# Query heads split one step ahead, and two small matmul groups set behind a denominator

## The chip, the cores and the metric

One core of a Trainium2 chip runs the whole program. The metric is device time in microseconds (us) of one execution; lower is better. PE is TensorE, ACT ScalarE, DVE VectorE, POOL GpSimd; SP only issues DMAs here. Each engine works through its own queue in order, and the engines wait for each other through semaphores.

## The reference, cut to what matters

```python
proj = q @ w_phi;  proj -= max(abs(proj), axis=-1)          # per head, 128 features
q_p = concat([exp(proj), exp(-proj)]);  k_p likewise
kv, z = k_p.T @ v, sum(k_p)                                 # per batch and head
x = (q_p @ kv) / (q_p @ z + 1e-6)                           # attention, 2304 tokens x 512
xn = x / sqrt(mean(x*x) + 1e-6) * rms_g
y = (silu(xn @ w_gate) * (xn @ w_val)) @ w_out              # feed-forward of width 1536
logits = y @ phi                                            # 32 slots
d = softmax of logits over tokens;  c = softmax over slots
slot_in = d.T @ y;  out = c @ experts(slot_in)              # soft mixture of 8 experts
```

## The kernel before

The work comes in three stages. In the first (to about 210 us) the keys are turned into features and `kv` and `z` are summed. The second is the feed-forward layer over six blocks of 384 tokens, and nearly all that the change touches lies in it. The third (from about 708 us) is the experts and the output.

In the second stage a block has 12 steps m. A step has three runs of matmuls on PE: the gate `pg` (12 matmuls of 384 columns), the value `pv` (12 again), and the output of the step before, `acc` (9 of 512 columns). After each of the three runs `fill()` is called; it runs whatever a list, `plan`, holds for that slot. So slot 3m lies behind the gate, slot 3m+1 behind the value, slot 3m+2 behind the output. Two kinds of work are put into these slots, by tables of numbers at the top of the file:

- `REDUCED` places the steps of `Reduced`, which makes the attention output of the next block (for blocks 2 to 5, so while blocks 1 to 4 run). Per head h: `split` (ACT casts the raw query to `qx`, DVE puts the remainder into the lower half), `feature` (two matmuls `qP`, an ACT copy into `qe`, a POOL maximum over the partitions), `exps` (DVE subtracts, ACT takes two exponentials). Per pair of heads c: `attend` (matmuls `num` with 64 columns of weights and `den` with 32, on DVE the reciprocal of `den`, eight small ACT copies that spread it, the product, the squares added into `s`). At the end `scale`: `ssq`, six passes of PE over `s`, then a reciprocal root on DVE, a sum on POOL, and `out`, whose result `xraw` is cast and split into `xnh` and `xnl` for the gate of the next block.
- `PSLOTS` places the nine steps of `post` for the block before: three turns `x2tp`, `logits` (`LT`, 32 columns of weights), `rows` (`L`), `dturn` (`dtp`), `dispatch` (`sps`, 32 columns), `combine` (DVE and ACT), `cturn` (`ctp`, then the copy `cb` on DVE and a DMA).

All of `qP`, `num`, `den`, `ssq`, `x2tp`, `LT`, `L`, `dtp`, `sps` and `ctp` take turns in three PSUM buffers of one tag. A framework compiles the program and may move an instruction some places forward or back on its engine; the order that comes out of it is quoted below. At the beginning `qx` has one buffer and `qraw` two, and `split(h + 1)` is written behind the matmuls of head h.

Of the kernel before, what the change touches and what calls it, by code (L numbers as in the profile page):

```python
# [7 lines left out]
F32 = mybir.dt.float32  # L8
F32R = mybir.dt.float32r
# [12 lines left out]
BLK = 384  # L22
# [6 lines left out]
NLEFT = 2  # L29
ELEFT = 4  # L30
CSKIP = 5
PSLOTS = [1, 4, 7, 10, 13, 15, 17, 19, 23]
REDUCED = [0, 0, 2, 3, 5, 6, 4, 8, 7, 11, 12, 9, 14, 12, 17, 18, 15, 20, 18, 23, 24, 26, 29]
TURNED0 = [2, 8, 14, 20, 12, 15, 20, 26, 28, 31]
TURNED1 = [0, 7, 14, 21, 6, 13, 20, 26, 28, 30]

# [25 lines left out]
def tile_kernel(ctx: ExitStack, tc: tile.TileContext, q2T, qT, kT, v, wbd, wg, wv, wo, rmsg, phi, w1, w2, consts, out):  # L62
# [34 lines left out]
    def split(hi, lo, src, hi_eng=None, lo_eng=None):  # L97

        if hi_eng is ACT:
            ACT.copy(out=hi, in_=src)  # L100
        else:
            (hi_eng or DVE).tensor_copy(hi, src)
        (lo_eng or POOL).tensor_tensor(out=lo, in0=src, in1=hi.bitcast(F32), op=ALU.subtract)  # L103
# [7 lines left out]
    class Conv:  # L111
# [6 lines left out]
        def load(self):  # L118
            j, nm, c = self.key
            self.raw = self.sp.tile([128, 512, 2], U32, tag="wraw", name="wraw", bufs=self.bufs[0])  # L120
            SP.dma_start(out=self.raw.rearrange("p n w -> p (n w)"), in_=wsrc[nm][j, :, 512 * c:512 * c + 512].bitcast(U32))
# [15 lines left out]
        def parts(self):  # L137
            j, nm, c = self.key
            if (nm, j) not in W:
                W[nm, j] = (wpA if j < 3 else wpool["B"]).tile([128, 2, 1024], F32R, tag="w", name=f"w{nm}{j}")  # L140
            u = W[nm, j]
            s = slice(512 * c, 512 * c + 512)
            split(u[:, 0, s], u[:, 1, s], self.w, hi_eng=ACT, lo_eng=POOL)
# [119 lines left out]
    class Reduced(Q):  # L263


        def load(self, h):
            if h < NH:
                self.raw[h] = self.sp.tile([128, BLK], F32, tag="raw", name="qraw", bufs=2)
                SP.dma_start(out=self.raw[h], in_=qT[self.blk - 2, h])

        def split(self, h):

            if h < NH:
                x = self.x[h] = self.sp.tile([128, BLK], F32R, tag="x", name="qx", bufs=1)
                ACT.copy(out=x, in_=self.raw[h])
                DVE.tensor_tensor(out=x[64:128], in0=self.raw[h][64:128], in1=x[64:128].bitcast(F32), op=ALU.subtract)  # L276

        def feature(self, h):
            x = self.x.pop(h)
            p = self.psum("qP", [128, BLK])  # L280
            PE.matmul(out=p, lhsT=ws, rhs=x, start=True, stop=False)  # L281
            PE.matmul(out=p, lhsT=wl, rhs=x, start=False, stop=True)
            e = self.e[h] = self.sp.tile([128, 2, BLK], F32, tag="e", name="qe", bufs=3)
            ACT.copy(out=e[:, 1], in_=p)  # L284
            POOL.partition_all_reduce(e[:, 0], e[:, 1], channels=128, reduce_op=bass_isa.ReduceOp.absmax)  # L285
            self.split(h + 1)
            self.load(h + 3)

        def exps(self, h):
            e = self.e[h]  # L290
# [10 lines left out]
            return r  # L301

        def begin(self):
            self.load(0)
            self.load(1)

        def steps(self):
            def first():
                self.split(0)
                self.load(2)  # L310

            f = [lambda h=h: self.feature(h) for h in range(NH)]
            a = [lambda c=c: self.attend(c) for c in range(4)]
            g = [lambda h=h: self.exps(h) for h in range(NH)]
            s = [first, *(x for c in range(4) for x in (f[2 * c], f[2 * c + 1], g[2 * c], g[2 * c + 1], a[c])), self.scale, self.out]
            return sorted(zip(REDUCED, s), key=lambda x: x[0])

    class Turned(Q):
# [7 lines left out]
        def split(self, c):  # L326
            if c < 4:
                xh = self.sp.tile([128, BLK], F32R, tag="xh", name="qxh", bufs=1)
                xl = self.sp.tile([128, BLK], F32R, tag="xl", name="qxl", bufs=1)
                split(xh, xl, self.raw[c], hi_eng=ACT)  # L330
                self.x = xh, xl
                self.load(c + self.bufs["raw"])
# [55 lines left out]
    with ExitStack() as pk:  # L388
# [5 lines left out]
        class Front:  # L394
# [10 lines left out]
            def split(self, hf):  # L405
                xh = self.sp.tile([128, 2, 128], F32R, tag=self.tag + "xh", name="xh", bufs=self.bufs["x"])
                xl = self.sp.tile([128, 2, 128], F32R, tag=self.tag + "xl", name="xl", bufs=self.bufs["x"])
                split(xh, xl, self.raw[:, 2 * hf:2 * hf + 2], hi_eng=ACT, lo_eng=DVE if self.i < 2 else POOL)
                self.x[hf] = xh, xl
# [225 lines left out]
    with ExitStack() as p2:  # L635
# [230 lines left out]
        for blk in range(NBLK):  # L866
# [25 lines left out]
            for n, f in qsteps:  # L892
                plan[n].append(f)
            for n, f in zip(PSLOTS, steps):
                plan[n].append(f)
# [189 lines left out]
```

## Time and profile before

| what | us |
|---|---|
| median of 3 runs (lowest, highest) | 775.92 (774.70, 778.17) |
| the profiled execution | 774.93 |
| its span, first to last instruction | 773.1 |
| PE busy in the span | 725.2 (94%) |
| DVE busy | 457.0 (59%) |
| ACT busy | 373.1 (48%) |
| POOL busy | 160.1 (21%) |

The granted TensorE clock over the whole span is 0.987. The share of PE is a mean over the three stages; what a wait in the second stage costs has to be read there. A matmul's record is longer than its distance from the next one, since matmuls overlap: a 384-column matmul is recorded with 0.34 us, and twelve follow each other in 2.12 us in the chain.

### The profile page before, as it was taken

The numbers are of one execution on the slowest core, as the hardware profiler recorded it, in microseconds if no ns is written. First come the engines' busy times: TensorE is split into PE (matmuls) and PEld (weight loads), VectorE is DVE, ScalarE is ACT, GpSimd is POOL, SyncE is SP. The second block draws the span as 40 slices with busy tenths as digits, with TensorE's granted clock in tenths as the row PEclk, the third lists the DMA queues.
The fourth block names the chain that finished last, engine by engine and source line by source line (L and its number), as shares of the span: only waits on it lengthen the run. The fifth ranks groups of instructions, "written<-read, shape, count | busy, mean of one in ns | idle before, by whom it ended". The sixth has DMA issues, their size and how long they took to land.

```text
span 773.1 us, 12571 instructions
## 1 busy us (share of the span) xinstructions
PE 725.2 (94%) x4871; PEld 580.3 (75%) x4871; DVE 457.0 (59%) x875; ACT 373.1 (48%) x867; POOL 160.1 (21%) x128
## 2 busy tenths in 40 slices
PE   6997899977899999999999999999999999999895
PEld 4664555966698887888878898789887899988343
DVE  6898777889956556455565555655556453423313
ACT  6889775565644455534555345553455531212102
POOL 2662330446610211012110121101211010000000
PEclk9999999999999999999999999999999999999899
DMA  8763311544201100101000010000100045667798
GB/s 282 246 209 101 125 42 50 194 137 162 84 23 36 32 21 21 46 1 32 21 20 19 1 32 22 22 19 1 32 21 1 8 162 216 222 218 284 285 374 289
DMA packets 27739, 79.47 MB, mean 103 GB/s; under 512 B 2976, under 2 KB 13664, under 8 KB 23584
## 3 DMA queue, kind: packets, MB, share of 16 engines
q1 hardware_dynamic: 27456, 77.79, 29.4%
q10 hardware_dynamic: 224, 0.88, 0.4%
q8 instruction: 38, 0.62, 0.3%
q14 instruction: 21, 0.17, 0.1%
HBM read 71.99 MB, written 6.67 MB: 102 GB/s over the span
## 4 chain that ended last, share of the span: by engine, by line
PE 65%; DVE 5%; ACT 4%; issue 1%; POOL 1%; DMA 0%; ACTq 0%; POOLq 0%; SPq 0%; DVEq 0%
PE pv L826 18%; PE pg L826 15%; PE acc L851 6%; PE acc L852 5%; PE acc L853 5%; PE num L213 3%; PE y L960 2%; PE y L976 2%; PE den L221 2%; ACT qe L231 1%; ACT e L231 1%; PE x2tp L654 1%; PE qP L281 1%; DVE qx L276 1%; DVE xraw L232 1%
## 5 line engine op out<-in xcount | busy, mean ns | idle before, releaser
L826 PE MATMUL pg<-xnh,wg 128*128 128x384 f32 x576 | 151.6, 343 | 0.9 <-ACT xnh L100 0.5
L826 PE MATMUL pv<-xnh,wv 128*128 128x384 f32 x576 | 151.1, 343 | 1.0 <-DVE t L838 1.0
L826 PEld LDWEIGHTS pg<-xnh,wg 128*128 128x128 f32 x576 | 104.5, 189 | 9.9 <-DVE hl L103 3.4
L826 PEld LDWEIGHTS pv<-xnh,wv 128*128 128x128 f32 x576 | 102.9, 188 | 6.7 <-issue 5.2
L285 POOL PARTITION_ALL_REDUCE qe<-qe x32 | 49.5, 1547 | 258.6 <-ACT qe L284 239.0
L826 PE MATMUL pg<-xnl,wg 128*128 128x384 f32 x288 | 97.7, 339 | 0.0
L826 PE MATMUL pv<-xnl,wv 128*128 128x384 f32 x288 | 97.7, 339 | 0.0
L851 PE MATMUL acc<-wo,hh 128*128 128x512 f32 x216 | 88.6, 410 | 2.1 <-ACT hh L100 2.1
L853 PE MATMUL acc<-wo,hl 128*128 128x512 f32 x216 | 85.8, 397 | 0.4 <-POOL hl L103 0.4
L852 PE MATMUL acc<-wo,hh 128*128 128x512 f32 x216 | 85.9, 398 | 0.0
L834 DVE SCALAR_TENSOR_TENSOR t<-t,pg 128x384 f32<-128x384 f32 x72 | 39.8, 553 | 62.9 <-ACT t L833 62.8
L833 ACT ACTIVATE t<-pg 128x384 f32<-128x384 f32 x72 | 35.0, 487 | 84.7 <-PE pg L826 84.6
L100 ACT CAST hh<-t 128x384 fp32r<-128x384 f32 x72 | 36.9, 512 | 72.7 <-PE acc L852 60.0
L103 DVE TENSOR_TENSOR hl<-t,hh 128x384 fp32r<-128x384 f32 x62 | 34.6, 558 | 47.4 <-ACT hh L100 41.6
L231 ACT COPY qe<-qe 32x192 f32<-32x192 f32 x128 | 44.8, 350 | 35.6 <-DVE qe L226 34.3
L838 DVE TENSOR_TENSOR t<-t,pv 128x384 f32<-128x384 f32 x72 | 39.6, 550 | 27.1 <-PE pv L826 26.2
L826 PEld LDWEIGHTS pg<-xnl,wg 128*128 128x128 f32 x288 | 54.3, 189 | 0.3 <-DVE xnl L103 0.2
L826 PEld LDWEIGHTS pv<-xnl,wv 128*128 128x128 f32 x288 | 54.0, 188 | 0.1
L851 PEld LDWEIGHTS acc<-wo,hh 128*128 128x128 f32 x216 | 41.0, 190 | 11.2 <-ACT hh L100 2.8
L465 PE MATMUL kacc<-kp,vt 128*64 128x256 f32 (+1 forms) x320 | 42.7, 393 | 6.8 <-ACT kp L442 6.8
L853 PEld LDWEIGHTS acc<-wo,hl 128*128 128x128 f32 x216 | 40.7, 188 | 10.9 <-POOL hl L103 1.0
L852 PEld LDWEIGHTS acc<-wo,hh 128*128 128x128 f32 x216 | 40.9, 189 | 6.4
(202 smaller groups left out, 1241.2 us busy)
## 6 DMA issues: line engine op xcount, KB each, us to landing
eu<-in_w_dram SPq DMA_DIRECT2D x32, 1024.0 KB, 6.2
wraw<-in_wg_dram SPq DMA_DIRECT2D x12, 512.0 KB, 4.4
wraw<-in_wv_dram SPq DMA_DIRECT2D x12, 512.0 KB, 4.2
wraw<-in_wo_dram SPq DMA_DIRECT2D x12, 512.0 KB, 4.3
qraw<-in_qT_dram SPq DMA_DIRECT2D x32, 192.0 KB, 2.4
raw<-in_kT_dram SPq DMA_DIRECT2D x18, 256.0 KB, 3.6
vt<-in_v_dram SPq DMA_DIRECT2D x18, 256.0 KB, 3.2
out_dram<-ob SPq DMA_DIRECT2D x18, 256.0 KB, 2.8
```

Source lines behind the costliest of these rows:

```text
L100: ACT.copy(out=hi, in_=src)
L103: (lo_eng or POOL).tensor_tensor(out=lo, in0=src, in1=hi.bitcast(F32), op=ALU.subtract)
L231: ACT.copy(out=rd[64 * hh + 32 * r:64 * hh + 32 * r + 32, g], in_=dn[o:o + 32])
L285: POOL.partition_all_reduce(e[:, 0], e[:, 1], channels=128, reduce_op=bass_isa.ReduceOp.absmax)
L465: PE.matmul(out=kva[o0:o0 + 64, hh // 2], lhsT=self.vt[r0:r1, h], rhs=kp[r0:r1, hh].rearrange("p s f -> p (s f)"), start=first and hh < 2, ...
L826: PE.matmul(out=p, lhsT=w[:, a, c], rhs=x, start=n == 0, stop=n == 11)
L833: ACT.activation(out=t, in_=g, func=AF.Tanh, scale=0.5)
L834: DVE.scalar_tensor_tensor(out=t, in0=t, scalar=1.0, in1=g, op0=ALU.add, op1=ALU.mult)
L838: DVE.tensor_tensor(out=t, in0=t, in1=wide("v", m, xs), op=ALU.mult)
L851: PE.matmul(out=acc[i], lhsT=hh[:, s], rhs=w[:, 0], start=m == 0, stop=False)
L852: PE.matmul(out=acc[i], lhsT=hh[:, s], rhs=w[:, 1], start=False, stop=False)
L853: PE.matmul(out=acc[i], lhsT=hl[:, s], rhs=w[:, 0], start=False, stop=m == MF - 1)
```

## The change

Three edits. First, `feature(h)` now begins with `split(h + 1)` and `load(h + 4)`, ahead of its own matmuls, and `qx` gets two buffers and `qraw` three; three heads are loaded at the begin of a block's queries in place of two. Second, in `REDUCED` the steps `scale` and `out` move from slots 26 and 29 to 27 and 30. Third, in `PSLOTS` the last six steps of `post` move: `logits` from 10 to 12 and `dispatch` from 17 to 18, which are the slots of the second and third `attend`; `rows` 13 to 14, `dturn` 15 to 16, `combine` 19 to 20, `cturn` 23 to 24, the slot of the last `attend`. In a slot the queries' steps come first.

```diff
-PSLOTS = [1, 4, 7, 10, 13, 15, 17, 19, 23]
-REDUCED = [0, 0, 2, 3, 5, 6, 4, 8, 7, 11, 12, 9, 14, 12, 17, 18, 15, 20, 18, 23, 24, 26, 29]
+PSLOTS = [1, 4, 7, 12, 14, 16, 18, 20, 24]
+REDUCED = [0, 0, 2, 3, 5, 6, 4, 8, 7, 11, 12, 9, 14, 12, 17, 18, 15, 20, 18, 23, 24, 27, 30]
...
-                self.raw[h] = self.sp.tile([128, BLK], F32, tag="raw", name="qraw", bufs=2)
+                self.raw[h] = self.sp.tile([128, BLK], F32, tag="raw", name="qraw", bufs=3)
...
-                x = self.x[h] = self.sp.tile([128, BLK], F32R, tag="x", name="qx", bufs=1)
+                x = self.x[h] = self.sp.tile([128, BLK], F32R, tag="x", name="qx", bufs=2)
...
         def feature(self, h):
             x = self.x.pop(h)
+            self.split(h + 1)
+            self.load(h + 4)
             p = self.psum("qP", [128, BLK])
...
             POOL.partition_all_reduce(e[:, 0], e[:, 1], channels=128, reduce_op=bass_isa.ReduceOp.absmax)
-            self.split(h + 1)
-            self.load(h + 3)
...
         def begin(self):
-            self.load(0)
-            self.load(1)
+            for h in range(3):
+                self.load(h)
...
                 self.split(0)
-                self.load(2)
+                self.load(3)
```

What the edits do to the order on the engines, at three places. First ACT, in the second block that makes reduced queries. Before, the cast for head 6 (`qx_4174`, seventh row) stands behind the eight copies of the second `attend` and the copy of head 5 (`qe_4171`):

```order
L223 COPY xraw_3932<-num_4106 128x384
L231 COPY qe_4001<-qe_3885 32x192 x8
L684 COPY c_4153<-L_4151 128x96
L100 CAST hh_4164<-t_4103 128x384
L238 ACTIVATE qe_4001<-xraw_3932 128x384
L284 COPY qe_4171<-qP_4168 128x384
L275 CAST qx_4174<-qraw_4007 128x384
L706 ACTIVATE c_4153<-c_4153 128x96
L833 ACTIVATE t_4190<-pg_4177 128x384
L284 COPY qe_4196<-qP_4193 128x384
```

Now the cast for head 5 is `qx_4027` and that for head 6 is `qx_4164`; `qe_4008` and `qe_4033` are the copies of heads 3 and 4:

```order
L100 CAST hh_3996<-t_3931 128x384
L235 ACTIVATE s_3961<-xraw_3934 128x384
L286 COPY qe_4008<-qP_4005 128x384
L275 CAST qx_4027<-qraw_3843 128x384
L833 ACTIVATE t_4024<-pg_4011 128x384
L286 COPY qe_4033<-qP_4030 128x384
L292 ACTIVATE qe_4008<-qe_4008 128x384
L275 CAST qx_4164<-qraw_3887 128x384
```

The cast for head 6 has moved from behind the second `attend` (slot 12) to a place ahead of it, behind the copy of head 4 (slot 9).

Second, PE where the logits stand, in the first block that makes reduced queries. Before, `LT` lies between a value and an output run:

```order
L826 MATMUL pv<-xnl_2835,wv_1552 128x384
L664 MATMUL LT<-x2T,phi_sb 32x128 x12
L851 MATMUL acc_2881<-wo_1149,hh 128x512
L852 MATMUL acc_2881<-wo_1149,hh 128x512
L853 MATMUL acc_2881<-wo_1149,hl 128x512
```

Now:

```order
L826 MATMUL pg<-xnl_2835,wg_1350 128x384
L213 MATMUL num<-qe,kv_1003 64x384 x4
L221 MATMUL den<-qe,kv_1003 32x192 x8
L664 MATMUL LT<-x2T,phi_sb 32x128 x12
L826 MATMUL pv<-xnh_2822,wv_1552 128x384 x2
```

`LT` has moved behind the second denominator; `sps` stands behind the third and `ctp` behind the fourth in the same way.

Third, DVE at the last `attend` of a block, before:

```order
L722 COPY cb_4384<-ctp_4380 96x384
L834 SCALAR_TENSOR_TENSOR t_4400<-t_4400,pg_4387 128x384
L225 TENSOR_SCALAR qe_4196<-den_4408 128x192
L226 RECIPROCAL qe_4196<-qe_4196 128x192
L838 TENSOR_TENSOR t_4400<-t_4400,pv_4431 128x384
L232 TENSOR_TENSOR xraw_3932<-xraw_3932,qe_4331 128x384
```

and now:

```order
L834 SCALAR_TENSOR_TENSOR t_4393<-t_4393,pg_4380 128x384
L225 TENSOR_SCALAR qe_4199<-den_4401 128x192
L722 COPY cb_4428<-ctp_4424 96x384
L226 RECIPROCAL qe_4199<-qe_4199 128x192
L838 TENSOR_TENSOR t_4393<-t_4393,pv_4431 128x384
L232 TENSOR_TENSOR xraw_3934<-xraw_3934,qe_4318 128x384
```

The copy `cb` has moved from ahead of the last denominator to between its addition and its reciprocal.

On SP, 13 query loads now stand ahead of the one load of `kv` in this stage, where it was 11, and that load has come ahead of a store of `cT_d` that it stood behind.

## Rows read from the trace of the kernel before

**Rows 1.** Windows: stretch, its length, busy PE, PEld, DVE, ACT, POOL, clock, DMA.

```profile
355.20:451.62 96.42, 94.29 (x562) 80.33 (x562) 54.04 (x107) 46.02 (x109) 14.88 (x9) 1.00 0.06 19
...
643.75:707.00 63.25, 63.25 (x356) 57.80 (x355) 20.78 (x45) 11.04 (x26) 0.00 (x0) 1.00 0.60 221
```

**Rows 2.** Waits of the run, PE behind DVE: us, times, longest.

```profile
PE qP L281 <- DVE qx L276: 6.5, 8, 1.2
...
PE ssq L248 <- DVE s L239: 3.3, 6, 0.7
```

**Rows 3.** PE by time, heads 4 and 6: start, length, operation, idle.

```profile
373.65 0.33 PE L826 MATMUL pg<-xnl,wg 128*128 128x384 f32 x1
374.43 0.44 PE L281 MATMUL qP<-qx,ws 128*128 128x384 f32 x1 [0.45 <-DVE qx L276]
374.71 0.34 PE L282 MATMUL qP<-qx,wl 128*128 128x384 f32 x1
...
391.48 0.33 PE L826 MATMUL pg<-xnl,wg 128*128 128x384 f32 x1
393.00 0.44 PE L281 MATMUL qP<-qx,ws 128*128 128x384 f32 x1 [1.19 <-DVE qx L276]
393.28 0.34 PE L282 MATMUL qP<-qx,wl 128*128 128x384 f32 x1
```

**Rows 4.** ACT by time, from the second attend to head 6.

```profile
386.72 2.88 ACT L231 COPY qe<-qe 32x192 f32<-32x192 f32 x8 [2.14 <-DVE qe L226]
...
390.74 0.46 ACT L284 COPY qe<-qP 128x384 f32<-128x384 f32 x1
391.10 0.52 ACT L275 CAST qx<-qraw 128x384 fp32r<-128x384 f32 x1
```

**Rows 5.** DVE by time, ahead of head 6.

```profile
391.38 0.97 DVE L705 TENSOR_TENSOR c<-c,rm 128x96 f32<-128x96 f32 x1
392.38 0.56 DVE L276 TENSOR_TENSOR qx<-qraw,qx 64x384 fp32r<-64x384 f32 x1
```

**Rows 6.** Chain of waits, pieces of the block: start, length, what.

```profile
377.17 1.00 PE LT L664 x24
378.17 0.43 PE acc L851
378.60 0.24 PE acc L852
...
380.47 2.11 PE pg L826 x12
...
384.82 2.31 PE pv L826 x12
...
397.95 0.99 PE sps L695 x6
398.94 2.31 PE pg L826 x12
...
414.60 0.33 PE ctp L720 x3
```

**Rows 7.** DVE by time, last attend of the block.

```profile
415.42 0.55 DVE L722 COPY cb<-ctp 96x384 f32<-96x384 f32 x1
...
419.35 0.36 DVE L225 TENSOR_SCALAR qe<-den 128x192 f32<-128x192 f32 x1 [1.18 <-PE den L221]
419.74 1.35 DVE L226 RECIPROCAL qe<-qe 128x192 f32<-128x192 f32 x1
```

**Rows 8.** PE by time, sums of squares of the block.

```profile
425.95 0.80 PE L248 MATMUL ssq<-small,s 128*128 128x1 f32 x6 [0.50 <-DVE s L239]
```

**Rows 9.** DVE by time, last split for the next block.

```profile
438.17 0.56 DVE L103 TENSOR_TENSOR xnl<-xraw,xnh 128x384 fp32r<-128x384 f32 x1
```

**Rows 10.** PE by time, last matmul of the next block's first gate.

```profile
439.57 0.34 PE L826 MATMUL pg<-xnl,wg 128*128 128x384 f32 x1
```

**Rows 11.** DMA issues of the page: transfer, count, KB, us to landing.

```profile
qraw<-in_qT_dram SPq DMA_DIRECT2D x32, 192.0 KB, 2.4
```

## The prediction

> **What bounds the kernel now.** I read the windows first. In a block of the second stage that also makes queries (355 to 452 us), PE is busy for 94.29 of 96.42 us at a clock of 1.00, while DVE has 54 and ACT 46; in the last block, which makes no queries, PE is busy without a gap (63.25 of 63.25) [rows 1]. So PE sets the time of this stage, and the 2.13 us in which it stood still are what can be won in such a block; an edit on another engine counts only through PE. Four blocks are like this one. The table of waits says for whom PE stood still: eight times for the remainder of a query head (`qx`, 6.5 us in all), so twice in each of the four blocks, and for the sums of squares `s` (6 times, 3.3 us; four of the six in these blocks) [rows 2]. PE in order of time shows where: at the `qP` of head 4 (0.45 us) and of head 6 (1.19 us) [rows 3], and at `ssq` (0.50 us) [rows 8]: 2.14 us together, the whole gap. DMA is no bound here (share 0.06).
>
> **Why heads 4 and 6 wait.** In both places the head before stands only one gate (2.11 us) ahead on PE, and with one `qx` buffer the cast of the next head cannot begin before that head's matmuls. For head 6 the rows show all links: ACT is held by the eight copies of the second `attend` until 389.60, copies head 5 at 390.74, casts head 6 at 391.10 [rows 4]; DVE is then still busy with the 0.97 us subtraction of `combine` and makes the remainder from 392.38 to 392.94 [rows 5]; PE starts at 393.00.
>
> **What the split one head ahead gives.** The loss is more than the idle time, because the stalled matmul and the next are also slower. I count from due to actual start of the second matmul of the head. A gate's matmuls follow each other every 2.11/12 = 0.176 us [rows 6]. Head 4: last gate matmul at 373.65, the second `qP` matmul due two places later, at 374.00, seen at 374.71: 0.71 us. Head 6: 391.48, due 391.83, seen 393.28: 1.45 us [rows 3]. Together 2.16 us a block, of which 0.26 us at each place is refilling. In the new order the cast for head 6 stands behind head 4's copy, and that for head 4 one head earlier in the same way, so each is queued a whole `attend` or more before its use: for head 6 about 16 us (391.5 less some 375) against a cast of 0.52 us and a DVE step of 0.56, or 0.97 as its neighbour took [rows 4, 5]. That leaves nothing of either wait; I take 2.16. Its ends are 0.71 (head 6 goes on waiting for something else) and 2.16.
>
> The edit moves work ahead of other work on two engines. On ACT each cast (0.52 us) stands ahead of exponentials and of the tanh, on DVE each remainder likewise. These have to be done before the next gate needs its PSUM buffer; since neither engine is busy for more than 54 of 96 us, a delay by one such step is covered, and I put it at nothing. If the cover were gone, it would be 0.5 us a block at one place. On SP two more query loads stand ahead of the one `kv` load, which is needed only two blocks later, and of the store of `cT_d`, which only the third stage reads. A load takes 2.4 us [rows 11] and is now asked for a head earlier, with three buffers: nothing.
>
> **What logits and dispatch behind a denominator give.** A run of matmuls that follows a group with narrow weights takes longer: the gate behind `sps` 2.31 us and the value behind `den` 2.31 us, against 2.11 us for a gate behind an output; the first output matmul behind `LT` 0.43 us, the next 0.24 [rows 6]. So each change back costs about 0.20 us (2.31 - 2.11 = 0.20; 0.43 - 0.24 = 0.19). `LT` and `sps` have 32 columns of weights like `den`. Directly behind it, their own 1.00 and 0.99 us remain, and one change back serves both: 0.19 + 0.20 = 0.39 us a block. Ends: 0 and 0.39; I take 0.39, as both kinds of row agree. The Trainium skill, page "TensorEngine Tiling (Array Packing)", section Tiling Modes, says that a change of tiling mode drains the array, and "TensorE: Matmul & The Clock Gate", Part 2, puts a drain at about 128 cycles, 53 ns at 2.4 GHz. By that estimate four switches a block fewer would give 0.21 us in place of 0.39, and the sum below would come out 0.7 us smaller (766.0 us); the rows, which have a duration for it, decide.
>
> `L`, `dtp` and `combine` move by one slot. The two on PE are one small pass each, before and after; what may change is the step of the run behind them, at most the 0.2 us that `acc` shows behind `LT`, up or down. I take 0. `ctp` (0.33 us) moves behind the last `den` and stays as long.
>
> **What the sums of squares a step later give.** Less than it looks. Before, `ssq` was due at 425.95 - 0.50 = 425.45 [rows 8]. Measured from the last denominator it is now due later by two gate matmuls (0.35 us: it stood in the middle of a gate) and by `ctp` (0.33 us), that is at 426.13, when `s` at its old time would be ready. But the change also puts the copy `cb` between DVE's addition and reciprocal of this denominator. Before, the reciprocal started at 419.74, right behind the addition that ended at 419.71 [rows 7]. The copy must wait for `ctp`, some 0.4 us behind the denominator, so about when the addition ends, and takes 0.55 us [rows 7]; the reciprocal starts 0.59 us later, and behind it stand the eight copies, the product, the square and the sum, one waiting for the other. `s` then comes for a start at 426.54, and PE waits 0.41 us in place of 0.50: a gain of 0.09 us. Ends: 0.50 + 0.26 = 0.76 if the wait goes, and -0.33 if the copy takes 0.97 like the step in [rows 5]. I take 0.09, since each link is a row.
>
> The end of this chain is the first gate of the next block. Its last input was ready at 438.73, and the matmul that reads it started at 439.57: 0.84 us of slack [rows 9, 10]. Behind the new `ssq` no two gate matmuls are left, so the slack falls by 0.35 to 0.49 us. It holds.
>
> `LT` now occupies one of the three PSUM buffers until ACT has taken its exponential, behind the eight copies. Head 6's `qP` wants that buffer. From the end of `den` PE has 1.00 (`LT`) + 2.31 + 2.11 (an output) + 0.35 (head 5) + 2.11 = 7.9 us to go; the copies begin 1.90 us behind it and last 2.88 us [rows 4, 6], and two activations of at most 0.52 us follow: 5.8 us. It holds with 2.1 us left.
>
> **Sum.** 2.16 + 0.39 + 0.09 = 2.64 us a block, four blocks: 10.6 us. Blocks without reduced queries gain nothing, and the third stage with the loads that the last block issues moves along. The profiled execution took 774.93 us: 764.3. It lay 0.99 us below the median; from the median, 775.92 - 10.6 = 765.3 us.
>
> **Rivals.**
> - The block's edge takes over. If two DVE steps between `ssq` and the last split take 0.97 in place of 0.56 us, the chain is 0.82 us longer than the slack of 0.49 allows: 0.33 + 0.26 us a block, 767.7 us. For it: the slack was cut; against: POOL makes one sum alone there, and the old times hold for the same steps. Chance 0.12.
> - Half: head 6 goes on waiting, now for a buffer. Then 0.71 + 0.39 + 0.09 = 1.19 us a block, 771.2 us. Against it stands the cover of 2.1 us. Chance 0.08.
> - The change doesn't do what it says: the casts stand earlier in the queue, but start no earlier, because their loads or buffers come no earlier. Only 0.48 us a block remain, 774.0 us. Against it: 2.4 us for a load, and head 4's matmuls are over 16 us before head 6 needs its own. Chance 0.10.
> - Slower: PE, which works in order, stops at head 6 until ACT has freed `LT`'s buffer. It costs nothing until ACT is 2.1 us later there than worked out; from then on each microsecond is lost in each of four blocks, and the gain is used up at 2.1 + 2.64 - 0.26 = 4.5 us. If ACT came to it 5.8 us late (two more runs of eight copies, 2.88 us each, ahead of it), it would cost 3.7 + 0.26 us a block: 775.92 - 10.6 + 15.8 = 781.1 us. Against it: nothing in the new order stands between those copies and the two activations. Chance 0.04.
>
> **Chances and range.** The forecast has 0.66. Faster by over 0.5% (below 772.0 us; about what a measurement of this kernel can tell from no change) are the forecast, the edge and the half: 0.86. Within 0.5%: 0.10. Slower: 0.04. The range holds the forecast with its ends and the edge. Low: with the `ssq` wait gone, 2.16 + 0.39 + 0.76 = 3.31 us a block, 762.7 us. High: nothing from the denominators and `ssq` at its worse end, 1.83 us a block, 768.6 us, and with 0.2 us a block for the moved `L` and `dtp` 769.4. With some tenths for the spread of the runs: 762.5 to 770.0.
>
> **What the profile after would show.** No wait of PE for `qx`; `ssq` still waiting for `s`, by about 0.4 us; `cb` between addition and reciprocal at the last denominator; the value behind `LT` and `sps` 2.31 us, and no long `acc` or gate elsewhere; blocks of about 93.8 us. It is wrong if PE waits at head 6 for ACT, or at a block's first gate for DVE by more than 0.3 us, or if blocks are above 95 us.

## The result, and the profile after

The changed kernel takes 762.61 us (median; 761.87 to 764.22), the kernel before, run beside it once more, 777.04 (774.70 to 778.25): a ratio of 0.983 with a 95% interval of 0.981 to 0.985, so 1.7% faster. The profiled execution took 764.22 us against 774.93, 10.7 less. The forecast was 765.3 in a range of 762.5 to 770.0.

Windows of the changed kernel, the same block as the first row of [rows 1]; columns as there:

```profile
358.50:451.83 93.33, 93.03 (x563) 80.75 (x562) 53.37 (x106) 46.02 (x109) 15.00 (x10) 1.00 0.07 19
```

The block takes 93.33 us in place of 96.42, and PE stands still for 0.30 in place of 2.13. POOL, ACT and DVE are busy for nearly as long as before; the clock is 1.00 in both. Four blocks are like this one: 4 × 3.09 = 12.4 us, more than the 10.6 forecast. The table of waits of the second stage, PE alone (us, times, longest), answers to [rows 2]:

```profile
PE ssq L248 <- DVE s L239: 1.2, 4, 0.3
```

There is no row for `qx` any more. The wait for `s` is shorter: in these four blocks the kernel before waits 2.0 us, 4 times (the 3.3 of [rows 2] has two waits of earlier blocks with it). The chain of waits in this block (start, length, what) shows the two heads that had waited, and the runs behind the denominators, which answer to [rows 3, 6], and `ssq`, to [rows 8]:

```profile
371.15 0.17 PE qP L283
...
379.27 0.79 PE den L221 x16
380.05 0.87 PE LT L664 x24
380.92 2.32 PE pv L826 x12
...
387.92 0.17 PE qP L283
...
396.95 0.85 PE sps L695 x6
397.80 2.31 PE pv L826 x12
...
412.48 0.79 PE den L221 x16
413.27 0.46 PE ctp L720 x3
413.73 2.11 PE pv L826 x12
...
420.35 0.83 PE ssq L248 x6
```

Heads 4 and 6 (371.15 and 387.92) follow the gate without a gap. `LT`, `sps` and `ctp` each stand directly behind a `den`, and the value behind `LT` and `sps` takes 2.31 us, as behind a bare `den` before. But `LT` itself now takes 0.87 and `sps` 0.85, where they took 1.00 and 0.99 [rows 6].

DVE in order of time at the last `attend`, which answers to [rows 7]:

```profile
413.33 0.36 DVE L225 TENSOR_SCALAR qe<-den 128x192 f32<-128x192 f32 x1 [1.18 <-PE den L221]
413.77 0.55 DVE L722 COPY cb<-ctp 96x384 f32<-96x384 f32 x1
414.24 1.34 DVE L226 RECIPROCAL qe<-qe 128x192 f32<-128x192 f32 x1
...
419.74 0.56 DVE L239 TENSOR_TENSOR s<-s,qe 128x384 f32<-128x384 f32 x1
```

The copy `cb` stands between addition and reciprocal. The reciprocal starts 0.97 us after the denominator's end in the chain (414.24 - 413.27); before it was 0.46 (419.74 - 419.28, the start of the value behind that `den`). That is 0.51 us later; the prediction had 0.59.

### The profile page after: what moved, and what is told of

Same layout as the page of the kernel before. It is cut to its first block, busy times and chain, and to the rows that moved or that the text cites. A ratio compares the mean times of both kernels' runs of the same rounds, so it can differ in the third digit from the quotient of the medians.

```text
span 762.4 us, 12573 instructions
## 1 busy us (share of the span) xinstructions
PE 722.6 (95%) x4871; PEld 583.3 (77%) x4871; DVE 453.7 (60%) x875; ACT 373.3 (49%) x867; POOL 160.8 (21%) x128
## 4 chain that ended last, share of the span: by engine, by line
PE 69%; ACT 1%; DVE 1%; issue 0%; ACTq 0%; DVEq 0%
PE pv L826 18%; PE pg L826 17%; PE acc L851 6%; PE acc L852 6%; PE acc L853 6%; PE num L213 3%; PE y L960 2%; PE y L976 2%; PE den L221 2%; PE x2tp L654 1%; PE qP L283 1%; PE qP L284 1%; PE op L997 1%; PE LT L664 1%; PE sps L695 1%; ACT qe L231 1%
## 5 line engine op out<-in xcount | busy, mean ns | idle before, releaser
L826 PE MATMUL pg<-xnh,wg 128*128 128x384 f32 x576 | 150.0, 342 | 0.9 <-ACT xnh L100 0.5
```

Of the source, the lines that this page charges most:

```text
L826: PE.matmul(out=p, lhsT=w[:, a, c], rhs=x, start=n == 0, stop=n == 11)
```

## The experiments

The sharpest measure is a block's length, the distance between the same instruction in two successive blocks of the profiled execution: it repeats to about 0.05 us from block to block (in `apart` to 0.4), while the whole time moves by some us from one execution to the next. `after_again`, `split_only`, `slots_only` and `cturn25` ran on one chip with the kernel before at 775.68 us (774.23 to 778.79), `buffers_only`, `ssq_only` and `cturn23` on another with it at 775.26 (773.50 to 777.53), `scale28` and `apart` on a third, one execution each, beside 775.0.

| kernel | median us | ratio to before (95%) | block us | against before |
|---|---|---|---|---|
| before | 775.68, 775.26 | | 96.42 | |
| `after_again` | 764.84 | 0.9855 (0.9831 to 0.9879) | 93.34 | -3.08 |
| `split_only` | 767.15 | 0.9884 (0.9861 to 0.9907) | 94.26 | -2.16 |
| `buffers_only` | 767.43 | 0.9894 (0.9879 to 0.9909) | 94.25 | -2.17 |
| `slots_only` | 769.75 | 0.9921 (0.9898 to 0.9943) | 95.02 | -1.40 |
| `ssq_only` | 773.79 | 0.9981 (0.9970 to 0.9993) | 96.06 | -0.36 |
| `cturn25` | 762.26 | 0.9822 (0.9800 to 0.9845) | 92.83 | -3.59 |
| `cturn23` | 763.74 | 0.9856 (0.9833 to 0.9880) | 93.24 | -3.18 |
| `scale28` | 766.24 | one execution | 94.35 | -2.07 |
| `apart` | 767.79 | one execution | 94.72 | -1.70 |

My theory after the result: the three edits act on PE alone, at places that the chain shows, and their sizes add up; what the sum had missed is the way into a narrow group. The rival: part of the difference is not in the edits but in how the two executions happened to run, or one edit only works because of another.

### The changed kernel once more

No edit.

> The changed kernel once more, beside the kernel before on one chip. Theory: the whole gain lies in the four blocks of the second stage, 96.42 to 93.33 us each, 12.4 us in all; what the medians differ by beyond that (14.4 us so far) is the spread of the runs. So the difference of the medians is 11.5 to 13.5 us, ratio 0.983 to 0.985. Rival: something outside these blocks became faster too; then the difference stays at 14 us or more, ratio 0.982 or less, and the first or third stage is shorter in the trace at the same granted clock.

The block took 93.34, 93.35 and 93.33 us (from `ssq` to `ssq`), the median 764.84, 10.8 below the kernel before on that chip. The gain of the blocks repeats to 0.02 us. The difference of the medians missed its forecast: it lies below the 11.5 to 13.5 expected, below the 14.4 of the first comparison and below the blocks' 12.4; the section on the prediction takes this up. The rival, a gain outside these blocks, has nothing for it.

### The split alone, and its buffers alone

`split_only` has the first edit and leaves both tables as they were:

```diff
 against the changed kernel
-PSLOTS = [1, 4, 7, 12, 14, 16, 18, 20, 24]
-REDUCED = [..., 27, 30]
+PSLOTS = [1, 4, 7, 10, 13, 15, 17, 19, 23]
+REDUCED = [..., 26, 29]
```

> The kernel before with the first edit alone: split one head ahead, two buffers for qx, three for qraw; both tables as before. Theory: both waits for qx go, 0.71 + 1.45 = 2.16 us a block, a block takes 94.2 to 94.4 us, the wait at the sums of squares stays 0.5 us; 8.6 us faster than the kernel before. Rival: without the moved tables head 6 still waits (DVE is busy with combine there); then 2 to 5 us faster.

The block is 2.16 us shorter, the term of the prediction to the digit. The only wait left on PE in these blocks is the one that the edit doesn't touch, 0.50 us each time:

```profile
PE ssq L248 <- DVE s L239: 2.0, 4, 0.5
```

`buffers_only` goes one step further back: the buffers and the earlier loads stay, but `split(h + 1)` is written behind the matmuls again:

```diff
 against split_only
         def feature(self, h):
             x = self.x.pop(h)
-            self.split(h + 1)
-            self.load(h + 4)
             p = self.psum("qP", [128, BLK])
...
             POOL.partition_all_reduce(e[:, 0], e[:, 1], channels=128, reduce_op=bass_isa.ReduceOp.absmax)
+            self.split(h + 1)
+            self.load(h + 4)
```

> The kernel before with more buffers alone (two for qx, three for qraw, loads a head earlier), but split written behind the matmuls of the head before, as it was. Theory: the second buffer is what takes the cast off the path, because the framework then moves the cast forward by itself; both waits go as in the kernel with the first edit whole: block 94.2 to 94.4 us, 8.6 us faster than before. Rival: the place in the text decides; the cast stays behind the copy of its head on ACT, head 4 or head 6 goes on waiting, and the gain is under 6 us.

It is the same as `split_only` (94.25 against 94.26). ACT in order of time:

```profile
374.23 0.50 ACT L275 CAST qx<-qraw 128x384 fp32r<-128x384 f32 x1
...
384.59 2.89 ACT L231 COPY qe<-qe 32x192 f32<-32x192 f32 x8 [2.14 <-DVE qe L226]
```

The cast for head 6 starts at 374.23, ahead of the eight copies of the second `attend`, though its line stands no earlier in the program than in the kernel before: with a free buffer the framework moves it forward. So it is the buffers that give the 2.16 us; once they are there, the place at which the split is written gives nothing more. The run keeps the third buffer of `qraw` and the earlier loads too, so it doesn't show the second buffer of `qx` by itself. The times of before speak for `qx`: the `qraw` buffer for head 6 came free with head 4's remainder at 374.37 (373.40 + 0.97), a load takes some 2.4 us [rows 11], and the cast began only at 391.10.

### The slots of the second table alone

```diff
 against the kernel before
-PSLOTS = [1, 4, 7, 10, 13, 15, 17, 19, 23]
+PSLOTS = [1, 4, 7, 12, 14, 16, 18, 20, 24]
```

> The kernel before with the third edit alone: the later slots for logits to cturn. Theory: LT and sps directly behind a denominator save 0.33 us each (no change of width before and behind them) and ctp 0.07; but cb now delays the last reciprocal by 0.51 us while ssq is due only 0.33 us later, so its wait grows from 0.50 to about 0.68 us: 0.55 us a block, block 95.9 us, 2.2 us faster, if the wait of head 6 stays. Rival: narrow groups cost the same wherever they stand; then no gain, 0 to 0.7 us slower. Open: the wait of head 6 (1.19 us) can change, since the steps of combine that stood before its remainder on DVE move too.

The block is 1.40 us shorter, where the narrow groups less the longer wait for `s` would give some 0.5; the case left open in the expectation came. PE still waits at both heads, but for less than in [rows 2]:

```profile
PE qP L281 <- DVE qx L276: 3.1, 8, 0.5
PE ssq L248 <- DVE s L239: 2.6, 4, 0.7
```

DVE in order of time shows where the rest comes from:

```profile
388.53 1.02 DVE L276 TENSOR_TENSOR qx<-qraw,qx 64x384 fp32r<-64x384 f32 x1 [0.17 <-ACT qx L275]
...
390.55 0.26 DVE L705 TENSOR_TENSOR c<-c,rm 128x96 f32<-128x96 f32 x1
```

The remainder for head 6 (L276, 388.53) now runs ahead of the subtraction of `combine` (L705, 390.55), which had held DVE in [rows 5], since `combine` moved from slot 19 to 20. That subtraction takes 0.26 us here and took 0.97 in [rows 5], where POOL's maximum for head 5 (L285) ran beside it from 391.29 to 392.87; the remainder, 1.02 us here, now runs beside that maximum (388.17 to 389.76). The cast comes earlier as well, 1.31 us ahead of the time at which the matmul is due (387.98 against 389.60 - 0.31) in place of 0.71 (391.10 against 393.00 - 1.19): PE now has the 0.87 us of `LT` to do between the denominator and head 6. The matmul of head 6 waited 0.31 us in place of 1.19: this edit takes 0.88 us of a wait that the first edit takes too. The wait for `s` grew from 0.50 to about 0.65, with the copy `cb` between addition and reciprocal, and `LT`, `sps` and `ctp` are as short as in the changed kernel.

### The sums of squares a step later, alone

```diff
 against the kernel before
-REDUCED = [..., 24, 26, 29]
+REDUCED = [..., 24, 27, 30]
```

> The kernel before with the second edit alone: scale and out one slot later. Theory: ssq is due two gate matmuls (0.35 us) later and s comes as before, so PE waits 0.15 us in place of 0.50; 0.35 us a block, 1.4 us faster, a step that the runs can just tell. Rival: the scale chain ends later at the block's edge (slack 0.84 us before) and the first gate of the next block waits for its last split; then no gain or slower.

The block is 0.36 us shorter, two gate matmuls (0.35). The table of waits has no row for `ssq` in these blocks any more, but the stall is not gone. The chain shows 0.13 us of "issue" between the end of the gate and `ssq`, and 0.80 us for `ssq`:

```profile
423.09 2.13 PE pg L826 x12
425.22 0.13 issue
425.35 0.80 PE ssq L248 x6
```

It is still a wait for `s`: `ssq` was due at 425.05 (the last gate matmul starts at 424.87, the next place is 0.18 later), DVE's sum into `s` ends at 425.20, and `ssq` starts 0.15 behind it. The matmuls' records are longer than their distance, so the gate's last one covers 0.17 of these 0.30 us and the chain shows 0.13.

### The copy `cb` out of the way, on either side

`cturn25` puts `ctp` and its copy one slot behind the last `attend`, so that `cb` stands behind the reciprocal; `cturn23` puts them one slot ahead, as before the change.

```diff
 against the changed kernel
-PSLOTS = [1, 4, 7, 12, 14, 16, 18, 20, 24]
+PSLOTS = [1, 4, 7, 12, 14, 16, 18, 20, 25]     cturn25
+PSLOTS = [1, 4, 7, 12, 14, 16, 18, 20, 23]     cturn23
```

> The changed kernel with the last step of the block before (ctp) one slot later, behind the value: slot 25 in place of 24. Theory: the 0.30 us for which PE still waits at the sums of squares come from the copy cb, which stands between the addition and the reciprocal of the last denominator; behind the reciprocal it costs nothing, the wait goes, and a block takes 92.8 to 93.0 us in place of 93.33: 1.2 to 2.2 us faster than the changed kernel. Rival: the wait comes from the chain behind the reciprocal alone; then PE goes on waiting 0.3 us and the block stays within 0.1 us of 93.33. Second rival: the copy then delays the next gate or value on DVE, and a wait at pg or pv appears.

> The changed kernel with ctp back in slot 23, ahead of the last gate and denominator; cb is then done before the denominator. Theory: the reciprocal starts as early as in the kernel before, ssq is due 0.35 us later than there: PE waits 0.1 to 0.2 us in place of 0.30, and ctp pays no change of width: block 93.1 to 93.3 us. Rival: the wait doesn't hang on cb and stays 0.3 us or more.

The chain of `cturn25`:

```profile
414.17 0.79 PE den L221 x16
414.96 2.31 PE pv L826 x12
417.27 0.33 PE ctp L720 x3
...
419.71 2.11 PE pg L826 x12
421.82 0.56 PE ssq L248 x6
```

and of `cturn23`, in both the stretch from the last `attend` to `ssq`:

```profile
415.81 0.79 PE den L221 x16
416.60 2.32 PE pv L826 x12
...
421.01 2.13 PE pg L826 x12
423.14 0.13 issue
423.27 0.80 PE ssq L248 x6
```

In `cturn25` PE does not wait at all: `ssq` starts at the gate's end and takes 0.56 us. The block is 0.51 us shorter than in the changed kernel, 92.83 as forecast; by its block this is the fastest of all these kernels. Its median, 762.26 us, is 2.6 below that of `after_again` on the same chip, but the runs of the two overlap (761.20 to 763.70 against 763.17 to 766.00), so the blocks show it and the medians alone don't. In `cturn23` no wait is recorded for `ssq`, but as in `ssq_only` there are 0.13 us of "issue" ahead of it and it takes 0.80: 0.37 us more than in `cturn25`, and the block is 0.40 longer. So 0.56 us is what `ssq` takes when PE comes to it without a stop, and behind a stop (0.13 to 0.50 us here) it takes 0.24 to 0.27 more, about the refill that the prediction counted at the heads (0.26). The whole price of the stop is then: before 0.50 + 0.24 = 0.74 [rows 8]; `ssq_only` 0.13 + 0.24 = 0.37; the changed kernel 0.30 + 0.27 = 0.57; `cturn25` nothing. The differences of these are the differences of the blocks: 0.74 - 0.37 = 0.37 for a measured 0.36, and 0.57 less the 0.07 that `ctp` costs by standing alone again, 0.50, for a measured 0.51.

### The logits and the dispatch one slot away from the denominators

```diff
 against the changed kernel
-PSLOTS = [1, 4, 7, 12, 14, 16, 18, 20, 24]
+PSLOTS = [1, 4, 7, 13, 14, 16, 17, 20, 24]
```

> The changed kernel with LT and sps set apart from the denominators again: logits in slot 13 (between value and output), dispatch in slot 17 (between output and gate); all else as changed. Theory: each group alone pays for a change of width before it (0.13 us) and behind it (0.20 us), behind a denominator it pays neither: a block takes 93.33 + 0.66 = 94.0 us. Rival, by the estimate that a switch is one drain of the array, 0.05 us, four of them: 93.5 us. Second rival: no cost of the place at all, 93.3 us.

The three blocks take 94.72, 94.73 and 94.30 us (from `sps` to `sps`), not the 94.0 expected; over the whole second stage it is 5.25 us more than in the changed kernel, 1.31 a block, twice what the narrow groups should cost. PE in order of time around `LT`, and at `sps`:

```profile
383.23 0.34 PE L826 MATMUL pv<-xnl,wv 128*128 128x384 f32 x1
383.49 1.07 PE L664 MATMUL LT<-x2T,phi_sb 128*32 128x128 f32 x24
384.50 0.50 PE L851 MATMUL acc<-wo,hh 128*128 128x512 f32 x1
384.83 0.40 PE L852 MATMUL acc<-wo,hh 128*128 128x512 f32 x1
```

```profile
394.78 1.06 PE L695 MATMUL sps<-x,d 128*32 128x512 f32 x6 [0.65 <-DVE d L690]
```

For `LT` the case is clean. From the start of `LT` to the second output matmul, less one regular output distance of 0.23 us, are 1.34 - 0.23 = 1.11 us; with the 0.09 by which `LT` starts later than the next value matmul would have (383.49 against 383.23 + 0.176) that is 1.19. Behind `den` it costs 0.87 (380.05 in the chain above). So standing alone costs 0.32 us, and two such groups, if `sps` costs the same, some 0.65 a block. At `sps` a new wait came in: one slot earlier `d` is not ready, and PE stands for 0.65 us here, 0.55 on average (2.2 us in 4). That is most of the other 0.66 us of the 1.31, and the block with the shortest of these waits (0.21 us) is the one of 94.30. The run gives the price of a narrow group for `LT` alone; for `sps` alone it doesn't.

### The sums of squares two steps later

```diff
 against the changed kernel
-REDUCED = [..., 24, 27, 30]
+REDUCED = [..., 24, 28, 31]
```

> The changed kernel with scale and out one more slot later, 28 and 31, that is behind the value. Theory: the chain from ssq to the last split for the next block had 0.57 us to spare in the changed kernel; moved by a value (2.12 us) it ends 1.0 to 1.6 us late (DVE does its gate and value steps ahead of the chain, which gives back up to 0.5), so the wait at ssq goes (0.56 us with refilling) and the first gate of the next block waits 1.0 to 1.6 us instead, with 0.26 of refilling: block 94.0 to 94.7 us. Rival: the edge has more room than the rows show; then only the gain is seen, 92.8 us.

The wait for `s` is gone, and the block is 1.0 us longer than in the changed kernel: 1.30 of a new wait and 0.26 of refill, less the 0.57 at `ssq`, as its expectation had it. Waits of PE and chain:

```profile
PE pg L826 <- DVE xnl L103: 5.2, 4, 1.3
```

```profile
422.13 0.56 PE ssq L248 x6
...
432.37 0.48 DVE xnl L103
...
432.89 2.03 PE pg L826 x10
```

PE in the first gate of the next block now waits 1.3 us for the last split `xnl`. It is the rival "the block's edge", which did not come in the changed kernel, and comes one step later: with 0.57 us of slack (below) `ssq` can move by less than a gate.

## Why the prediction was right, and where it was off

**The sum of the block.** The chains of before and after give, a block: the heads 2.16; `LT` from 1.00 + 0.20 to 0.87, 0.33; `sps` likewise from 0.99 + 0.20 to 0.85, 0.34; `ctp` with the value behind it from 0.33 + 2.31 to 0.46 + 2.11, 0.07 (the prediction had put nothing here); the stop at `ssq` with its refill 0.17 (0.74 less 0.57). That is 3.07 for a measured 3.09.

**The heads** were right to the digit, and alone (`split_only`). The count from due to actual start, with the refill, was the right one: the idle time alone would have given 1.64. The prediction named the single `qx` buffer as what held the cast back, but told the gain as one of the new order; `buffers_only` shows that with the buffers there the written place adds nothing. The cast for head 6 starts 15 us ahead of its matmul in the changed kernel:

```profile
372.81 0.50 ACT L275 CAST qx<-qraw 128x384 fp32r<-128x384 f32 x1
...
381.90 2.88 ACT L231 COPY qe<-qe 32x192 f32<-32x192 f32 x8 [0.66 <-DVE qe L226]
...
385.01 0.35 ACT L676 ACTIVATE dT<-LT,nM_run 96x128 f32<-96x128 f32 x1
```

**The narrow groups** are the term that was mis-sized: 0.39 in the sum, 0.67 measured. The prediction took only the way out (the run behind the group, 0.20) and said that the group's "own 1.00 and 0.99 us remain". They don't: behind another narrow group they are 0.13 and 0.14 shorter, so the way in costs as well, and `LT` alone in `apart` gives 0.32 for both together. The rows ahead of the prediction couldn't show this directly, but the bound should have been open upwards: 0 and 0.39 were its ends, and the value lay outside. The estimate from the Trainium skill ("TensorE: Matmul & The Clock Gate", Part 2, a drain of about 128 cycles; "TensorEngine Tiling (Array Packing)", Tiling Modes, on the drain at a change of mode), 0.21 a block, is a third of what the runs show.

**The sums of squares** gained 0.20 of waiting and not 0.09. The finding that the copy `cb` would eat most of the gain was right: `cturn25`, with `cb` behind the reciprocal, wins 0.51 a block more, and `ssq_only`, where `cb` stays ahead of the denominator, wins 0.36. The size of the delay was 0.51 and not 0.59, because the reciprocal's record begins before the copy's ends (414.24 against 413.77 + 0.55); that accounts for 0.08 of the 0.11. Two more differences nearly cancel. `ssq` is due 0.61 us later, not 0.68, because the value behind `ctp` is shorter (due 6.17 us behind the denominator before, 425.45 - 419.28, and 6.78 now, 420.05 - 413.27). And `ssq` starts 0.05 us behind the end of `s`, where it was 0.14 before (425.95 against 425.25 + 0.56); why, the runs don't show.

**What was put at nothing.** The block's edge: DVE's last split ends at 433.06 and the matmul that reads it starts at 433.63, 0.57 us of slack where 0.49 was worked out and 0.84 stood before [rows 9, 10].

```profile
432.52 0.54 DVE L103 TENSOR_TENSOR xnl<-xraw,xnh 128x384 fp32r<-128x384 f32 x1
```

```profile
433.63 0.34 PE L826 MATMUL pg<-xnl,wg 128*128 128x384 f32 x1
```

`LT`'s PSUM buffer: ACT's activation `dT` ends at 385.36, 5.3 us after the denominator's end at 380.05; 5.8 was worked out, against a cover of 7.9. Neither the slower rival nor the half came. Casts and remainders ahead of other work cost nothing that PE shows: no wait for `pg` or `pv` stands in the table.

**The edits don't add up, and why.** Alone they give 2.16, 1.40 and 0.36, together 3.92, but 3.09 in one kernel. The first and the third both take 0.88 us of head 6's wait, which can be taken once: 3.92 - 0.88 = 3.04, 0.05 short of the measured.

**The whole time.** Four blocks are 12.4 us, and the profiled execution gained 10.7. I cut each trace at the sums of squares near 236 us and at the first `x2tp` behind the last block:

| profiled execution | to 236 us | second stage | third stage |
|---|---|---|---|
| before | 236.14 | 477.44 | 59.52 |
| after | 236.38 | 465.06 | 60.96 |
| `after_again` | 237.75 | 465.11 | 61.04 |
| `cturn25` | 238.57 | 463.07 | 59.96 |
| `split_only` | 235.02 | 468.78 | 60.00 |
| `buffers_only` | 236.89 | 468.77 | 61.04 |

The second stage holds the gain and repeats to 0.05 us. The first varies from 235.0 to 239.5 and the third from 59.5 to 61.1 over all eleven traces, also between kernels that are the same there. For the third stage the profiles show what varies. The chain of before, from the sums of the slots to the output:

```profile
721.09 1.09 PE stp L791 x8
...
725.13 10.59 PE y L960 x74
```

and of after:

```profile
708.95 1.93 PE stp L791 x8
...
713.83 11.18 PE y L960 x74
```

The same eight matmuls `stp` take 1.09 us in one and 1.93 in the other, and the windows of the first 12 us of this stage (the number before the last two is the clock) give a granted clock of 0.85 and 0.80:

```profile
713.58:725.58 12.00, 8.71 (x65) 5.26 (x67) 7.37 (x30) 3.01 (x11) 0.95 (x1) 0.85 0.73 286
```

```profile
701.44:713.44 12.00, 8.79 (x61) 5.87 (x59) 6.98 (x29) 3.02 (x11) 0.95 (x1) 0.80 0.74 296
```

Both are means between the two levels, 0.50 (1.2 GHz) and 1.00 (2.4 GHz). `stp` itself ran at the upper level in the kernel before and at the lower one in the changed kernel:

```profile
721.09:722.18 1.09, 1.07 (x8) 0.96 (x8) 0.85 (x5) 0.28 (x2) 0.00 (x0) 0.95 1.06 451
```

```profile
708.95:710.88 1.93, 1.91 (x8) 1.77 (x8) 0.86 (x5) 0.44 (x2) 0.00 (x0) 0.50 0.90 382
```

In both kernels PE was busy for 6.3 to 6.4 of the 7.51 us from the start of the stage to `stp`. In the kernel before the clock fell behind `stp` and was at 1.00 again from 729 us on, after some 7 us; in the changed kernel it had begun to fall ahead of `stp` (0.79 from 708.00 to 708.95) and was at 1.00 again from 719 us on, after some 10 us. Over all eleven traces the two go together: a clock of 0.80 or 0.81 in these first 12 us with a third stage of 60.96 to 61.06 us (`after`, `after_again`, `buffers_only`, `cturn23`), 0.85 to 0.91 with 59.5 to 60.3 (the other seven). Whether the change itself also shifts this clock is not settled: the low one came in both profiled executions of the changed kernel, but also in `buffers_only`, and not in `cturn25` or `split_only`.

"The third stage moves along" was therefore not exact for a single execution, by 1.44 us, and this and the 1.8 us too little in the blocks nearly cancelled: that 764.3 was forecast for the profiled execution and 764.22 came is luck. The median of 762.61 lies inside the range by only 0.11 us, and not because of a term of the sum: the blocks' 12.4 us off the 775.92 of the prediction give 763.5. Of the medians' difference, 14.4 us in the first comparison and 10.8 in the second, the blocks explain 12.4. The rest, 2.0 too much and 1.6 too little, is of the size by which the two outer stages vary; the executions without a trace can't be taken apart to show it.

## What to carry to other kernels

Count a stall from the due to the actual start of the second instruction behind it, and ask of a wait first whether a second buffer removes it; here the order then followed by itself. Small groups of matmuls with narrow weights gained here by standing next to each other, since each one alone paid on the way in and on the way out (0.32 to 0.34 us). A copy that was moved next to a chain on DVE cost nearly its full length on that chain (0.51 of 0.55 us): where PE is the bound, look at what stands between the instruction that PE waits for and its releaser, and move the copy behind it.

## What the runs showed of the hardware that was not expected

A group of matmuls with 32 columns of weights between runs with 128 columns cost 0.32 to 0.34 us more than its place directly behind another 32-column group: 0.13 to 0.14 of it in the group's own chain length (`LT` 1.00 against 0.87, `sps` 0.99 against 0.85), 0.20 in the run behind. A stop of PE of 0.13 us left no row in the table of waits and no idle time at its instruction: in `ssq_only` and `cturn23` it shows only as "issue" in the chain, and yet cost 0.37 us, since six tiny matmuls took 0.80 us behind it in place of 0.56.
